# Turning the last normalized rows by DMA, and three shifts of order, in a long forward and backward kernel

## The chip, the cores and the metric

The kernel runs on one core of a Trainium2 chip. The metric is device time in microseconds (us). Before the change three runs took 1935.72, 1935.73 and 1937.65 us, median 1935.73. The run whose profile is shown took 1934.85 us; its span, from the first to the last instruction, is 1933.1 us, at a granted TensorE clock of 0.999.

The core has five engines that run in parallel, each through its own list of instructions in order: PE (TensorE, matmuls), DVE (VectorE) and ACT (ScalarE) for elementwise work, POOL (GpSimd) and SP (SyncE), which here mostly issue transfers. Transfers run on 16 DMA engines. An instruction that needs another engine's result waits for a semaphore, and everything behind it on its own engine waits with it.

## The reference, cut to what matters

The forward pass over x (2048 rows of 1024, bf16) is

```
xn = layernorm(x)
kv = shift(k) * v                     # shift: 4 taps per channel along the rows
y  = causal_conv(kv, ssm_k) + kv * D  # length 2048, by FFT in the reference
s  = xn * y
bm = ((xn @ w_gate) * (xn @ w_up)) @ w_down
out = x + s * silu(bm)
```

The kernel must give `out` and the gradients with respect to x, k, v, the shift taps, ssm_k, D and the three weight matrices for a given grad_out. The widths are 1024 model channels and 3584 inner channels.

## The kernel before, in words

The 2048 rows are 16 blocks of 128. Weights and activations stay bf16; sums are in PSUM, in f32.

**First stage, layer norm.** The rows come in six groups, `chunks`: one block, one, two, and then three groups of four (first blocks 4, 8 and 12). `ln_load` loads a group's rows on SP's queue, `layer_norm` takes mean and variance on DVE, a root on ACT, and normalizes in place (L584, L582, L585). The normalized rows lie with rows on the partitions; the matmuls need the 1024 channels on the partitions. So each block is turned: eight 128x128 transposes on PE (L591 for the first two blocks, L599 for the others) into a PSUM tile `tr`, and a copy from there into `XNT`, alternately on ACT (L601) and on DVE (L603). XNT is four tiles of four blocks; it lies in the big buffers U0 to U3, which the profile, like all of these, calls U. The rows of the three groups of four lie in U4, U6 and U7 until other data take these buffers. SP also stores turned h (below).

**Gate and up projections.** `gu_unit` takes a slab of 256 inner channels and a group of blocks: per block eight matmuls of 128x512 into `psg` (L642), a cast to `gut` by ACT (L644), and a store. The product of both halves, `hN`, is made on DVE a unit later, stored by POOL, and some units later turned on PE (L669), copied on ACT (L670) and stored by SP as `HTd`. There are 14 slabs. Slabs 0 and 1 are partly worked while the layer norm still runs; slab 1 on the last two groups, and all others, come after it, and call `tick` after each block.

**Forward convolution.** It is a generator, `conv_forward`, whose pieces are mixed into the projections. Channels go in eight blocks `ds` of 128. For every second ds, `shift` forms kv of 256 channels on DVE from k and v (loaded by POOL), in eight steps of 2.3 us; its running sum takes U6. The transforms of kv and of ssm_k are matmuls with cosine and sine tables (`psF`, L235), copied to `SP` tiles by ACT (L257, L295), and combined on DVE (tiles W, KX, HX); then a product, and an inverse transform (`inv_dft`, or `inv8` for ds 2 and 5), whose sums are on DVE and whose matmuls are `psY`. The first half-transforms of the next ds (`half`, two calls) are put on PE's list by `ahead`, once in the middle of the inverse transform (`mid`) and once behind its second reading (`after_read`), about one DVE step later. The name SP stands both for this tile and for the engine SyncE; the text says which.

`tick` counts blocks from -5, and `pump` advances the generator to the share of its planned cost that belongs to the count; from count 0 on it follows the blocks. These costs only set the order in which instructions are written out. Once they are written, each engine runs its own list, and in this stage the lists of the convolution are kept in that order.

**What comes after.** Down projection (`psbm`), gating of the output, and the backward passes of the projections, the convolution and the layer norm follow, with their own generator for the backward convolution. The change doesn't touch them.

Of the kernel before, what the change touches and what calls it, by code (L numbers as in the profile page):

```python
# [19 lines left out]
def build_kernel(  # L20
# [11 lines left out]
    nc = tc.nc  # L32
    P = 128
# [11 lines left out]
    def nat(ap2d):  # L45
        return ap2d.rearrange("(c u r) d -> u c r d", c=2, u=P, r=8)

    xq = nat(A_q.flatten_outer_dims())
# [11 lines left out]
    def ld(out, in_):  # L60
        return nc.sync.dma_start(out=out, in_=in_)
# [3 lines left out]
    def st(out, in_):  # L65
        ins = nc.gpsimd.dma_start(out=out, in_=in_)  # L66
        if PINQ[0]:
            tc.keep_in_program_order(ins)
        return ins
# [17 lines left out]
    def pool(name, bufs=1, side=None, space=None):  # L87
        kw = dict(name=name, bufs=bufs, reuse_waits="tile")
        if side:
            kw["side"] = side  # L90
        if space is not None:
            kw["space"] = space
        return tc.alloc_tile_pool(**kw)
# [118 lines left out]
    def tt(o, a, b, op):  # L212
        pinned(V.tensor_tensor(o, a, b, op))  # L213
# [292 lines left out]
    def u8(i, pat="p (a x) -> p a x", **kw):  # L506
        return U[i][:].rearrange(pat, **kw)

    XNT = [u8(q, a=DC) for q in range(4)]
# [9 lines left out]
    def keep_busy(n):  # L519
        for i in range(n):  # L520
            mm = nc.tensor.matmul(busy[:, i % 4, :], ident[:], ident[:], start=True, stop=True)
        return mm
# [19 lines left out]

    def ln_load(b0, n, x4):
        c, r0 = divmod(b0, 8)
        ld(x4[:, 0:n, :], xq[:, c, r0:r0 + n, :])

    tr_ln, act_copy = [None], [None]

    def layer_norm(b0, n, x4):
        def small(name, dt=F32):  # L550
            return lns.tile([P, 4], dt, name=name)[:, 0:n]
        mv = lns.tile([P, 4, 2], F32, name="mv")[:, 0:n, :]
        for i in range(n):
            bst = lns.tile([P, 2, 6], F32, name="bst")
            for hh in range(2):
                V.bn_stats(out=bst[:, hh, :], in_=x4[:, i, hh * 512:(hh + 1) * 512])  # L556
            V.bn_aggr(out=mv[:, i, :], in_=bst[:])
        var_b = small("var_b", BF16)
        V.tensor_copy(var_b, mv[:, :, 1])
        vpe = small("vpe", BF16)  # L560
        V.tensor_scalar(vpe, var_b, EPS, None, op0=ADD)
        r0_ = small("r0_")
        with tc.issue_after(act_copy[0].ins) if act_copy[0] is not None else nullcontext():
            root = nc.scalar.activation(r0_, vpe, ACT.Sqrt)
        mean_b = small("mean_b", BF16)
        V.tensor_copy(mean_b, mv[:, :, 0])
        rr0 = small("rr0")
        V.reciprocal(rr0, r0_)
        mean_f = small("mean_f")
        V.tensor_scalar(mean_f, mean_b, -1.0, None, op0=MUL)  # L570
        q0 = small("q0")
        tt(q0, vpe, rr0, MUL)
        r1 = small("r1")
        tt(r1, r0_, q0, ADD)
        sq_b = small("sq_b", BF16)
        V.tensor_scalar(sq_b, r1, 0.5, None, op0=MUL)
        V.reciprocal(RSTD[:, b0:b0 + n], sq_b)
        for i in range(n):
            b = b0 + i
            q, qi = divmod(b, 4)  # L580
            if n == 4 and i < 2:
                nc.scalar.activation(x4[:, i, :], x4[:, i, :], ACT.Identity, bias=mean_f[:, i:i + 1])  # L582
            else:
                V.tensor_scalar(x4[:, i, :], x4[:, i, :], mean_f[:, i:i + 1], None, op0=ADD)  # L584
            last = V.tensor_scalar(x4[:, i, :], x4[:, i, :], RSTD[:, b:b + 1], None, op0=MUL)  # L585
            if b < 2:
                for hh in range(2):
                    ps = ps_st.tile([P, 4, P], BF16, name="tr")
                    for dc in range(4):
                        d0 = (4 * hh + dc) * P  # L590
                        tr_ln[0] = nc.tensor.transpose(ps[:, dc, :], x4[:, i, d0:d0 + P], ident[:])  # L591
                    act_copy[0] = nc.scalar.copy(out=XNT[0][:, 4 * hh:4 * hh + 4, b * P:b * P + P], in_=ps[:])
                if b == 0:
                    with tc.issue_after(tr_ln[0].ins):
                        keep_busy(10)
                continue
            ps = ps_st.tile([P, DC, P], BF16, name="tr")
            for dc in range(DC):
                tr_ln[0] = nc.tensor.transpose(ps[:, dc, :], x4[:, i, dc * P:(dc + 1) * P], ident[:])  # L599
            if i % 2 == 0:  # L600
                act_copy[0] = nc.scalar.copy(out=XNT[q][:, :, qi * P:(qi + 1) * P], in_=ps[:])  # L601
            else:
                V.tensor_copy(XNT[q][:, :, qi * P:(qi + 1) * P], ps[:])  # L603
        c, r0 = divmod(b0, 8)
        return last, root, st(xnn[:, c, r0:r0 + n, :], x4[:, 0:n, :])
# [69 lines left out]
    INV8 = (2, 5)  # L675
# [4 lines left out]
    def conv_forward():  # L680
        S_ = conv_state

        def load_kv(dp, c):
            S_["k", dp] = krow
            if dp > 0 or c == 0:
                for i in range(2) if dp == 0 else (c,):
                    cld_k(krow[:, i], i, dp)
            if dp > 0 or c == 1:
                for i in range(2) if dp == 0 else (c,):
                    v = U[4][:, 2048 * i:2048 * i + 2048].rearrange("p (a x) -> p a x", a=8)  # L690
                    cld_v(v, i, dp * 256, 256)
# [43 lines left out]
        def kvs(ds):  # L735
            return S_["kvt", ds // 2][:, :, ds % 2 * P:(ds % 2 + 1) * P]
# [17 lines left out]
        cs = pool("cs", 1)  # L754
# [4 lines left out]
        def half(ds, x, i, first=None):  # L759
            if (ds, int(first is not None)) not in EIGHT:  # L760
                return fwd4_half(x, i, cf, ps_cv, first)
            SP = cf.tile([P, 2, 2, 512], F32, name="SP", bufs=2)
            fwd8_half(x, i, SP, ps_cv, first, True)
            return SP
# [34 lines left out]
        for ds in range(8):  # L799
            yield 0.5  # L800
            if ds % 2 == 1 and ds < 7:
                with tc.issue_after(S_["kst"].ins):
                    for c in range(2):
                        load_kv(ds // 2 + 1, c)
            D0 = Dz[:, ds * P:(ds + 1) * P]
            sph = []
            KX = cx.tile([P, 16, 256], BF16, name="KX")
            HX = cs.tile([P, 16, 256], BF16, name="HX", bufs=2)
            own_room = lambda X: X[:].rearrange("p a x -> p (a x)").bitcast(F32).rearrange("p (a x) -> p a x", a=8)[:, 0:4]
            eight = (ds, 1) in EIGHT  # L810
            if ds == 0:
                yield from transform(0, 1, sp, HX, own_room(KX), lambda i: sph.append(half(0, kvs(0), i)), nop)
            else:
                yield from transform(ds, 0, sp, KX, own_room(HX), lambda i: sph.append(half(ds, S_["hx"], i, D0)), nop)
                S_["kst"] = st(KFd[ds], KX[:])
            next(tl, None)
            room = cf.tile([P, 4, 256], F32, name="room", tag="hx")[:] if eight else None
            yield from transform(ds, int(ds > 0), sph, HX if ds else KX, room, nop1 if eight else lambda c: h_rows(ds + 1, c),
                                 lambda: next(tl, None))
            if ds == 0:  # L820
                S_["kst"] = st(KFd[0], KX[:])
            if eight:
                h_rows(ds + 1, 0)
            turned(HX, 1, 0, 1)
            yield 1.3
            if eight:
                h_rows(ds + 1, 1)
            if ds == 7:
                cf.release()
                S_["forward"] = False  # L830
            st(HFd[ds], HX[:])
            yield from product(KX, HX, KX, cs, False, 0)
            if ds % 2 == 1 and ds < 7:
                yield from shift(ds // 2 + 1)
            sp = []

            def ahead():
                if ds < 7:
                    sp.append(half(ds + 1, kvs(ds + 1), len(sp)))
            yield from (inv8 if ds in INV8 else inv_dft)(KX, HX, cs, ahead, ahead)  # L840
            S_["G", ds] = HX
            tl = tail(ds)
        yield 6.0
# [62 lines left out]
    cnt = [-5]  # L906
    NT = 24 * 8.0 + 14

    def tick(by=1):
        cnt[0] += by  # L910
        if cnt[0] == -4:
            pump((SHIFT_W + 4.05) / F_TOTAL)
        if cnt[0] >= 0:
            pump((SHIFT_W + (F_TOTAL - SHIFT_W) * (cnt[0] + 5) / (NT + 2)) / F_TOTAL)

    pump((SHIFT_W + 3.95) / F_TOTAL)
# [341 lines left out]
    for bp in range(1, 8):  # L1258
        ht, ht_ld = load_ht(bp) if bp > 2 else (ht1, ht2)[bp - 1]
        if bp in (3, 5, 7):  # L1260
            q = (bp - 3) // 2
# [361 lines left out]
```

## Time and profile before

| | busy us | share of the span |
|---|---|---|
| PE | 1909.7 | 99% |
| DVE | 1542.9 | 80% |
| ACT | 639.1 | 33% |
| POOL | 329.0 | 17% |

The table is the mean of stages with different limits. In the first 60 us, layer norm and first slabs, PE is busy 53.66 us and DVE 56.15; from 320 to 540 us, projections with convolution, 218.01 and 210.60 of 220; from 540 to 1300 us, 758.92 and 613.09 of 760. A wait in the profile's lists is time in which an engine stood idle until the named producer had finished. Matmuls are pipelined: one of 128x512 is listed with 379 ns, but a run of eight takes 1.73 us, 216 ns each. DMA lines give the time from issue to landing, which contains waiting behind other transfers.

### The profile page before, as it was taken

The page shows a single profiled execution, that of the slowest core. Times are in us where ns is not written, and L with a number is a line of the kernel's source. Part 1 is how long each engine was busy: PE and PEld are TensorE (multiplying, and loading weights), DVE is VectorE, ACT ScalarE, POOL GpSimd, SP SyncE. Part 2 cuts the span into 40 slices and gives each one's busy share as a digit, 9 for nine tenths or more (in the row PEclk, how much of TensorE's full clock was granted, in tenths as well). Part 3 has the DMA queues.
Part 4 walks back from the last instruction along what each step waited for, and adds up shares of the span by engine and source line. Part 5 has one row for each costly group of instructions (what it writes and reads, how often), then busy time and mean ns, then how long its engine had stood idle before and what let it go on. Part 6 is the DMA issues. An engine that isn't in the chain of part 4 may idle for free.

```text
span 1933.1 us, 27373 instructions
## 1 busy us (share of the span) xinstructions
PE 1909.7 (99%) x10860; PEld 1033.0 (53%) x10994; DVE 1542.9 (80%) x1720; ACT 639.1 (33%) x942; POOL 329.0 (17%) x461
## 2 busy tenths in 40 slices
PE   8999999999999999999999999999999999999999
PEld 5555555555544447666666666664444444444444
DVE  9999999999937555888899999999996403388883
ACT  5854555556423224333222222221222102011113
POOL 4121211201112220000122122021121101011111
PEclk9999999999999999999999999999999999999999
DMA  8876765767979987666788788575787999889873
GB/s 294 265 243 223 254 212 195 253 212 264 309 215 324 311 271 263 213 216 197 265 249 258 242 241 277 186 275 187 213 255 176 167 206 212 154 183 189 191 204 132
DMA packets 451216, 444.43 MB, mean 230 GB/s; under 512 B 268784, under 2 KB 371340, under 8 KB 436624
## 3 DMA queue, kind: packets, MB, share of 16 engines
q1 hardware_dynamic: 394704, 243.36, 46.8%
q0 software_dynamic: 40064, 169.95, 27.3%
q10 hardware_dynamic: 16320, 29.36, 4.1%
q8 instruction: 86, 1.41, 0.3%
q14 instruction: 42, 0.34, 0.1%
HBM read 194.00 MB, written 185.64 MB: 196 GB/s over the span
## 4 chain that ended last, share of the span: by engine, by line
PE 88%; DVE 9%; issue 2%; ACT 1%; DMA 0%; DVEq 0%; ACTq 0%
PE psb L1331 20%; PE psx L1461 20%; PE psg L642 12%; PE psb L1314 10%; PE psbm L961 10%; PE psb L1409 9%; PE psF L235 3%; DVE W L213 2%; DVE U L213 1%; DVE KX L213 1%; DVE bst L556 1%; PE psY L438 1%; PE tr L669 1%; PE psY L449 1%; PE psY L1108 1%
## 5 line engine op out<-in xcount | busy, mean ns | idle before, releaser
L642 PE MATMUL psg<-wslab,U 128*128 128x512 bf16 x1735 | 401.8, 379 | 3.8 <-ACT U L644 0.5
L1331 PE MATMUL psb<-U,U 128*128 128x512 bf16 x1792 | 397.1, 379 | 0.0
L1461 PE MATMUL psx<-U,dgut 128*128 128x512 bf16 x1505 | 331.0, 379 | 1.6
L1461 PEld LDWEIGHTS <-dgut 128*128 128x128 bf16 x1792 | 175.3, 98 | 211.4
L1331 PEld LDWEIGHTS <-U 128*128 128x128 bf16 x1792 | 175.3, 98 | 198.0
L642 PEld LDWEIGHTS <-U 128*128 128x128 bf16 x1792 | 173.0, 98 | 186.5 <-issue 1.9
L1314 PE MATMUL psb<-wdt,U 128*128 128x256 bf16 x1792 | 205.6, 273 | 0.0
L1314 PEld LDWEIGHTS <-U 128*128 128x128 bf16 x1792 | 175.3, 98 | 29.2
L1409 PE MATMUL psb<-U,U 128*128 128x512 bf16 x797 | 175.9, 379 | 0.9
L1336 ACT CAST wb<-psb 128x512 bf16<-128x512 f32 x112 | 65.5, 585 | 315.5 <-PE psb L1331 304.8
L213 DVE TENSOR_TENSOR W<-W 128x1024 f32<-128x1024 f32 (+1 forms) x168 | 165.4, 1001 | 3.6
L961 PE MATMUL psbm<-U,ht 128*128 128x512 bf16 x658 | 145.0, 379 | 0.7
L1409 PEld LDWEIGHTS <-U 128*128 128x128 bf16 x896 | 87.5, 98 | 104.5
L644 ACT CAST gut<-psg 128x512 bf16<-128x512 f32 x156 | 91.1, 587 | 129.1 <-PE psg L642 124.7
L1493 ACT ACTIVATE dx_t<-dxn 128x1024 bf16<-128x1024 f32 x15 | 15.9, 1057 | 320.1 <-DVE dxn L213 320.1
L961 PEld LDWEIGHTS <-ht 128*128 128x128 bf16 x672 | 65.6, 98 | 78.6
L213 DVE TENSOR_TENSOR U<-U,dht 128x2048 bf16<-128x2048 bf16 x56 | 68.3, 1221 | 47.0 <-ACT dht L1316 46.9
L1160 DVE SCALAR_TENSOR_TENSOR dkp<-dkT,kT 128x1024 bf16<-128x1024 bf16 (+2 forms) x64 | 78.4, 1224 | 32.6 <-DMA dkT<-DKSHd 30.8
L1316 ACT CAST dht<-psb 128x512 bf16<-128x512 f32 x112 | 65.6, 586 | 116.4 <-PE psb L1314 116.4
L213 DVE TENSOR_TENSOR dxn<-psx,dxna_t 128x1024 f32<-128x1024 f32 x15 | 18.3, 1222 | 85.6 <-PE psx L1461 82.4
L66 POOL DMA_DIRECT2D Hd<-hN x54 | 37.1, 688 | 264.8 <-DVE hN L213 262.4
L1440 ACT CAST wbs<-psb 128x512 bf16<-128x512 f32 x51 | 29.8, 585 | 145.1 <-PE psb L1409 134.1
(256 smaller groups left out, 2464.6 us busy)
## 6 DMA issues: line engine op xcount, KB each, us to landing
U<-GUd SPq DMA_DIRECT2D x28, 1024.0 KB, 7.5
DGd<-U SPq DMA_DIRECT2D x28, 1024.0 KB, 5.3
GUd<-gut ACTq DMA_DIRECT2D x39, 512.0 KB, 6.4
out_dram<-wb SPq DMA_DIRECT2D x112, 128.0 KB, 4.0
U<-Hd SPq DMA_DIRECT2D x14, 1024.0 KB, 6.7
Hd<-hN POOLq DMA_DIRECT2D x54, 256.0 KB, 5.0
HTd<-hT SPq DMA_DIRECT2D x52, 256.0 KB, 3.6
ht<-HTd SPq DMA_DIRECT2D x6, 1536.0 KB, 10.9
```

Of the source, the lines that this page charges most:

```text
L213: pinned(V.tensor_tensor(o, a, b, op))
L235: mm = nc.tensor.matmul(ps[:, k].rearrange("p (c d) -> p c d", c=2), T[:, r, k, :], xr[:, r], start=(n == 0), stop=(n == len(rs) - 1 and ( ...
L642: gu_mm[0] = nc.tensor.matmul(ps[:], XNT[q][:, dc, qi * P:(qi + 1) * P], w[:, dc].rearrange("p a f -> p (a f)"), start=(dc == 0), stop=(dc ...
L644: nc.scalar.copy(out=gut[:, :, i], in_=ps[:].rearrange("p (a f) -> p a f", a=2))
L961: mm = nc.tensor.matmul(ps[:, dh * 512:(dh + 1) * 512], ht(fc)[:, i * P:(i + 1) * P], WD[fc // 4][:, fc % 4, dh * 512:(dh + 1) * 512], sta ...
L1160: ins = V.scalar_tensor_tensor(prod[:].rearrange("p r d -> p (r d)")[:, lo:H], dkT[:, 0, lo:H], 1.0, kT[:, 0, 13 + m + lo:13 + m + H], op0 ...
L1314: nc.tensor.matmul(ps[:, x * SLW:(x + 1) * SLW], DBMT[2 * hf + g][:, dc, (b % 4) * P:(b % 4 + 1) * P], wdt[:, dc, :], start=(dc == 0), sto ...
L1316: nc.scalar.copy(out=dht[:, 2 * e:2 * e + 2].rearrange("p b f -> p (b f)"), in_=ps[:])
L1331: nc.tensor.matmul(ps[:], XN[b // 4][:, b % 4, dc * P:(dc + 1) * P], dgus[b // 8][:, :, b % 8], start=(b == 0), stop=(b == NB - 1))
L1336: nc.scalar.copy(out=wb[:, dc % 2].rearrange("p a f -> p (a f)"), in_=ps[:])
L1409: nc.tensor.matmul(ps, h[:, f, b, :], DBM[b // 4][:, b % 4, dh * 512:(dh + 1) * 512], start=(b == 0), stop=(b == NB - 1))
L1461: nc.tensor.matmul(ps[:, dh * 512:(dh + 1) * 512], t[n][:, f, i * P:(i + 1) * P], WGU[n][:, f, dh * 512:(dh + 1) * 512], start=(n == 0 and ...
```

## The change

Four edits:

1. The first block of rows is loaded as two transfers of 512 columns each, in place of one.
2. For the fifth and sixth groups of rows (b0 of 8 and 12), the eight transposes on PE and the copy of every block are left out. In their place stands one transposing DMA per block on SP's queue, from the normalized rows in SBUF to XNT in SBUF: eight transfers of 128x1024 bf16.
3. For odd ds, those whose next ds works on a freshly shifted kv, the first half-transform is no longer put on the list at `mid` but at `after_read`, and the second one after the end of the inverse transform.
4. `pump` follows the blocks from count -2 in place of 0.

```diff
 def ln_load(b0, n, x4):
     c, r0 = divmod(b0, 8)
-    ld(x4[:, 0:n, :], xq[:, c, r0:r0 + n, :])
+    if b0 == 0:
+        for hh in range(2):
+            ld(x4[:, 0, hh * 512:hh * 512 + 512], xq[:, c, 0, hh * 512:hh * 512 + 512])
+    else:
+        ld(x4[:, 0:n, :], xq[:, c, r0:r0 + n, :])
...
             continue
+        if b0 >= 8:
+            nc.sync.dma_start_transpose(out=XNT[q][:, :, qi * P:(qi + 1) * P], in_=x4[:, i, :])
+            continue
         ps = ps_st.tile([P, DC, P], BF16, name="tr")
...
-        yield from (inv8 if ds in INV8 else inv_dft)(KX, HX, cs, ahead, ahead)
+        yield from (inv8 if ds in INV8 else inv_dft)(KX, HX, cs, ahead if ds % 2 == 0 else None, ahead)
+        if ds % 2 == 1:
+            ahead()
...
-    if cnt[0] >= 0:
+    if cnt[0] >= -2:
         pump((SHIFT_W + (F_TOTAL - SHIFT_W) * (cnt[0] + 5) / (NT + 2)) / F_TOTAL)
```

## The prediction

> **What bounds the kernel now.** I read the page first, then the windows by stage, then the waits of PE, then the timeline of PE and of DVE around the places that the change touches, last the DMA issues.
>
> ```profile
> PE 1909.7 (99%) x10860; PEld 1033.0 (53%) x10994; DVE 1542.9 (80%) x1720; ACT 639.1 (33%) x942; POOL 329.0 (17%) x461
> ...
> 0.00:60.00 60.00, 53.66 (x395) 31.38 (x401) 56.15 (x155) 36.46 (x58) 27.23 (x43) 1.00 0.91 304
> ...
> 180.00:200.00 20.00, 17.62 (x95) 9.66 (x95) 18.45 (x13) 8.96 (x12) 2.57 (x4) 0.91 0.52 177
> ...
> 320.00:540.00 220.00, 218.01 (x1320) 121.21 (x1343) 210.60 (x195) 116.98 (x166) 32.75 (x46) 1.00 0.75 252
> 540.00:1300.00 760.00, 758.92 (x4601) 447.66 (x4618) 613.09 (x671) 228.64 (x341) 129.99 (x183) 1.00 0.77 250
> ```
>
> The first line is busy time of each engine over the span of 1933.1 us: PE has only 23.4 us in which it does nothing. The windows (stretch, then busy time of PE, PEld, DVE, ACT, POOL, then clock, DMA share, GB/s) say where these lie: 6.3 us in the first 60, 2.4 in 180:200, almost none after 540. So behind 540 us nothing is to be had except by moving everything earlier, and what the change does before 540 moves all that follows by the same amount. But DVE is busy 56.15 of 60 and 210.60 of 220 there: from 53.6 to 533 us it runs the shift and the forward convolution almost without a break. PE and DVE limit this stage together, and one cannot run far ahead of the other.
>
> ```profile
> PE psF L235 <- DVE kv L213: 3.2, 2, 2.3
> PE tr L599 <- DVE U L585: 2.3, 4, 0.8
> ...
> 36.39 0.39 PE L669 MATMUL tr<-ident,hN_s 128*128 128x128 bf16 x4
> 37.49 0.62 PE L599 MATMUL tr<-ident,U 128*128 128x128 bf16 x8 [0.71 <-DVE U L585]
> 37.95 0.38 PE L642 MATMUL psg<-wslab,U 128*128 128x512 bf16 x1
> 38.28 1.51 PE L599 MATMUL tr<-ident,U 128*128 128x128 bf16 x24
> 39.85 3.19 PE L642 MATMUL psg<-wslab,U 128*128 128x512 bf16 x14
> ...
> 48.43 0.62 PE L599 MATMUL tr<-ident,U 128*128 128x128 bf16 x8 [0.64 <-DVE U L585]
> 48.88 0.38 PE L642 MATMUL psg<-wslab,U 128*128 128x512 bf16 x1
> 49.22 1.51 PE L599 MATMUL tr<-ident,U 128*128 128x128 bf16 x24
> ```
>
> The first two lines are PE's waits (total us, times, longest): the matmuls on a freshly shifted kv, and the transposes that wait for a normalized row. The rest is PE's timeline around the last two groups of rows: start, length, what, and in brackets PE's idle time.
>
> **What the Trainium skill says.** "VectorE: DVE Perf Modes", section "The three transpose paths", gives 390 ns for TensorE and 1309 ns for the DMA crossbar, both for one 128x128 block. The trace has the TensorE ones pipelined, 24 in the 1.57 us from 38.28 to 39.85, 65 ns each. "Advanced Engine Details and Errata", section "X-Bar Transpose (TRN2)", calls transposing DMAs as fast as ordinary ones. The trace has them only from DRAM (dkT, as large as one block of rows here: issue 1.29 us, landing 3.6 us); none reads SBUF. "DMA: Bandwidth & Descriptors", section "Queues, rings and completion order", has each DMA engine go round the queues that have work, a packet at a time, so a transpose on SP's queue shares with POOL's loads. The trace agrees: small stores of SP land very late in this stretch.
>
> ```profile
> HTd<-hT_s SPq DMA_DIRECT2D x2, 128.0 KB, 9.1
> k<-in_A_k_dram POOLq DMA_DIRECT2D x4, 704.0 KB, 10.5
> dkT<-DKSHd SPq DMA_TRANSPOSE x16, 3.6
> ...
> 53.61 2.29 DVE L213 TENSOR_TENSOR U<-k,Wbc 128x4096 bf16<-128x4096 bf16 x1
> ...
> 72.45 0.69 DVE L213 TENSOR_TENSOR hN<-gut 128x1024 bf16<-128x1024 bf16 x1
> 76.94 0.69 DVE L213 TENSOR_TENSOR hN<-gut 128x1024 bf16<-128x1024 bf16 x1 [3.81 <-ACT gut L644]
> ```
>
> (DMA lines: KB each, median us from issue to landing; dkT has no size there, its tile is 128x1024 bf16, 256 KB.)
>
> **The change, part by part.**
>
> *First rows in halves.* DVE starts its first statistics at 3.60 us, 1.17 us after it ran dry, waiting for the load. Half the data lands a little sooner; against that SP spends another 0.43 us of issue before the weight slabs. The start is a chain on DVE (17.07 us busy of the first 20), so what DVE gains moves on, while a slab 0.4 us later is absorbed by PE's waits for DVE just behind. Bounds: 0.5 us won, 0.2 lost; I take 0.3 won.
>
> *Transposes of the last two groups.* PE loses 64 transposes. In the timeline they fill 37.49 to 37.95, 38.28 to 39.85, 48.43 to 48.88 and 49.22 to 50.78: 4.0 us, and the waits in front, 0.71 and 0.64, go too. Together 5.4 us. DVE loses four copies of 0.68 us (2.7), ACT four of 1.0.
>
> What is added: eight transposing DMAs on SP, in the order of SP's queue after the fourth and after the sixth store of turned h. The last two groups are the fifth and sixth of rows. The first four wait for rows that DVE normalizes from 36.94 to 38.6, then take at least 1.3 us each. PE needs these rows only after the 64 matmuls of the group before: it began them at 48.43 less the wait and five matmuls, 46.7 us, so at 44 us without the group's own transposes and wait (2.7), and then a row every 1.73 us (8 matmuls). Landing at about 40 to 47, they are in time. The second four follow rows normalized from 47.88 on; two copies fewer and the earlier start make it 46.4. PE began its matmuls on them at 57.41 and had done the four blocks at 64.31; without stall it now begins at 57.4 - 5.7 = 51.7. But from 46 to 58 us POOL's k and v loads fill the DMA engines (share 1.04 in that window; 0.33 in 38:40). A store of 128 KB on SP took 9.1 us there. Good end: first landing at 53, the rest 1.3 us apart; PE then ends the group at 53 + 4 x 1.73 = 59.9, 4.4 earlier than before. Bad end: first landing 46.4 + 9 = 55.4, then half the engines, 2.6 us each, so 63.2 for the fourth and 64.9 for the end, 0.6 later than before. I take the middle, 1.9 us earlier: of 5.7 us won, 3.8 come back as PE waiting for the DMA.
>
> Behind these on SP stand stores of turned h (nobody waits soon) and the third slab's load, issued at 64.51 when its buffer comes free: no loss.
>
> The same 2 MB also delay others. k's last load landed at 53.3 in the trace, just ahead of DVE's first shift multiply at 53.61. Eight transposes are some 10 us of all engines; I let k land 1 to 4 us later. The first shift multiply also overwrites the fifth group's x buffer, now read by DMA; those should have landed by 47. POOL waits for k too (4.77 us, until 50.58), with the stores of the products hN behind it, which nobody misses for some us. DVE could start at 50.6 and starts at about 56; kv, 18.9 us on, ends near 75. There is some room: DVE stood idle 3.81 us at 73.1 in any case. PE reached the kv matmuls at 78.20. In the new order they stand some 2.2 us sooner and PE is 1.9 earlier: 74.1. So about 0.9 us of new wait.
>
> *Pace sooner.* The order of DVE now has the first sums W ahead of the product hN, for which it idled those 3.81 us. This costs no instruction, and fills that gap with work of the 480 us chain. It wins PE nothing by itself; it lets DVE follow a PE that comes earlier. I book 0.5 us of the small waits around 75 to 85. Zero is the low end, 1 the high one.
>
> *Transforms one step later.* Behind the shift, the two halves for the next channel block are put on PE's order one and two DVE steps later (2.3 and 2.8 us), behind more psg matmuls. The wait for kv was 2.3 at 187 and about 1 at 306: 3.2 us in total, of which nearly all goes. The danger is the other end: DVE needs the first half's result right behind the inverse transform. It was PE that ran ahead at these places, by 2.3 us and more, so the result should be there. Bounds: 3.2 won, or 1 if DVE waits instead; I take 3.2.
>
> *Sum.* 0.3 + 1.9 - 0.9 + 0.5 + 3.2 = 5.0 us off the profiled span, 1933.1 to 1928.1. The run that was profiled took 1934.85, and the three timed ones have a median of 1935.73; the same 5.0 off that median is 1930.7 us.
>
> **The rivals.**
>
> A. Everything lands in time: 0.3 + 5.4 + 3.2 + 0.5 = 9.4 us, 1926.3 us. For it: the DMA share of 0.33 in 38:40, enough for the first group. Against: 46 to 58 us, as above.
>
> B. DVE becomes the bound. The transposes give nothing, k comes 4 us late, and the won kv waits turn into PE waiting for hN or for the sums, since DVE has only 14 us without work between 53 and 533 (465.71 busy of 480). Then nothing to 2 us remain: 1934.5 us. For it: that figure. Against: 2.7 us of copies leave DVE, and the 3.81 us gap is fillable.
>
> C. Slower: an SBUF source makes the crossbar slow. The eight queue on SP one behind another from 37 us. With s us each, the last lands at 37 + 8s + 2 and PE ends the group 1.7 later. Against 64.3 before, and with 3.5 won elsewhere, it decides at s = 3.4 us. By the skill's 1309 ns for each of eight blocks in a row s would be 10.5 and the loss over 50 us; dkT's landings, eight such blocks in 3.6 us, speak against that, so if it comes I expect s near 5: the last at 79, PE 16 us late, 1948 us.
>
> That the change doesn't do what it says is excluded for the transposes: the new order of PE has 64 fewer.
>
> **How the numbers follow.** Chances: the forecast 0.38 (1927.5 to 1933), A 0.27 (1924 to 1928), B 0.22 (1932 to 1938), C 0.13. Some 0.2%, 3.9 us, is what a measurement of this kernel can tell from no change. All of A and nearly 0.9 of the forecast's case lie below 1931.9: 0.60. Within: the rest of the forecast's and most of B: 0.23. Slower: C and the upper end of B: 0.17. Range: from A's middle less its uncertainty to B's end, 1924.5 to 1938.0, C left out.
>
> **What the profile after would show.** No transposes of groups five and six on PE (64 fewer); DMA_TRANSPOSE on SP at 37 to 52 us. If I am right: PE waits for them (releaser DMA U<-U) of 3 to 5 us, only on the last group; the kv wait below 0.5 us; DVE's 3.8 us idle before hN gone; k's landing near 56. If A: no such wait. If C: SP issues of over 3 us each. I am wrong if PE shows new waits on SP (the tile), W or hN in 80 to 530 us that add up to over 3 us, or if DVE idles after the inverse transforms.

## The result, and the profile after

The changed kernel took 1955.53 us (median of four runs, 1953.29 to 1959.11), beside 1935.72 us for the kernel before on the same chip (four runs, 1935.56 to 1937.65). The ratio is 1.0102, with a 95% interval of 1.0084 to 1.0119: some 20 us slower, where 5 us faster was forecast. The profiled span is 1951.5 us against 1933.1, 18.4 longer.

The page first: the engines' busy time, the granted clock in 40 slices, and PE's costliest group in this stage (busy us and mean ns, then idle us before it and what ended most of it). The last line is the same group before the change.

```profile
PE 1909.0 (98%) x10796; PEld 1029.0 (53%) x10930; DVE 1541.4 (79%) x1716; ACT 635.5 (33%) x938; POOL 329.9 (17%) x461
...
PEclk9799999999999999999999999999999999999999
...
L649 PE MATMUL psg<-wslab,U 128*128 128x512 bf16 x1735 | 405.5, 383 | 27.3 <-DMA U<-U 18.7
```

```profile
L642 PE MATMUL psg<-wslab,U 128*128 128x512 bf16 x1735 | 401.8, 379 | 3.8 <-ACT U L644 0.5
```

PE has lost its 64 transposes, from 10860 to 10796 instructions, yet is busy for as long as before. The last two lines say why: the matmuls that consume the turned rows cost 405.5 us in place of 401.8, and PE stood idle 27.3 us in front of them where before it was 3.8. Of these, 18.7 wait for `U<-U`, the new DMA. The clock has a 7 in the second slice of 49 us, so part of these matmuls ran slower.

PE's and DVE's waits give the number of times and the longest.

```profile
PE psg L649 <- DMA U<-U: 18.7, 3, 11.5
PE psg L649 <- ACT gut L651: 4.5, 2, 3.4
```

```profile
DVE U L213 <- DMA U<-U: 22.1, 1, 22.1
```

The waits for kv (3.2 us before) no longer stand in PE's list. Two new ones do: the transposing DMAs, and a wait for a cast of 3.4 us at about 534 us, as long as the kv waits were together. DVE waits for the DMAs too, once, for 22.1 us. The timeline of SP's own queue shows where the transfers stood (start, length, what).

```profile
37.40 28.36 SPq L602 DMA_TRANSPOSE U<-U  x4
65.86 1.07 SPq L61 DMA_DIRECT2D HTd<-hT_s  x2
67.02 9.99 SPq L602 DMA_TRANSPOSE U<-U  x4
77.11 2.26 SPq L61 DMA_DIRECT2D HTd<-hT_s  x2
83.05 0.37 SPq L540 DMA_DIRECT2D wslab<-in_B_w_up_dram  x1
```

To issue the first four transposes took SP 28.36 us, 7 us each. They were issued at 37.40, 39.02, 41.66 and 53.97 and landed at 43.0, 58.3, 69.6 and 73.5. The second four, for rows that had been normalized by 48.6, could not be issued until 67.02; they landed at 75.2 to 80.9. The view of this source line has the shortest, the median and the longest issue in ns:

```profile
L602 SPq DMA_TRANSPOSE U<-U x8: 1255/2052/12217, 37.4 to 75.7; - x8
```

The shortest are the last three, 1.25 to 1.33 us each at 73 to 77 us; the longest are the third and the fourth, about 12 us each. The timelines of PE and of DVE show what that did.

```profile
41.55 5.34 PE L649 MATMUL psg<-wslab,U 128*128 128x512 bf16 x24
58.37 3.59 PE L649 MATMUL psg<-wslab,U 128*128 128x512 bf16 x8 [11.48 <-DMA U<-U]
61.76 1.06 PE L676 MATMUL tr<-ident,hN 128*128 128x128 bf16 x8
...
69.68 0.61 PE L649 MATMUL psg<-wslab,U 128*128 128x512 bf16 x1 [6.86 <-DMA U<-U]
...
73.55 1.90 PE L649 MATMUL psg<-wslab,U 128*128 128x512 bf16 x8 [0.31 <-DMA U<-U]
...
82.86 0.22 PE L733 MATMUL tr<-ident,U 128*128 128x128 bf16 x1
```

```profile
51.00 0.68 DVE L174 TENSOR_SCALAR mm<-mm 128x1024 int32<-128x1024 int32 x1
73.82 2.29 DVE L213 TENSOR_TENSOR U<-k,Wbc 128x4096 bf16<-128x4096 bf16 x1 [22.13 <-DMA U<-U]
```

PE resumes each time a block lands: 58.3, 69.6, 73.5. All three are blocks of the first four; PE does not wait for the second four. The last line of PE's is the same place in the work as one before the change, the transposes that follow the last group's matmuls:

```profile
64.31 0.22 PE L726 MATMUL tr<-ident,U 128*128 128x128 bf16 x1
```

82.86 less 64.31 is 18.5 us, and the spans differ by 18.4. So all of the loss is made by 83 us, and behind that point nothing is earned or lost in sum: the kv waits of 3.2 us are gone, and the 3.4 us at 534 have come. DVE's wait has a second cause in the same transfers: the shift's first multiply writes into U6, which holds the fifth group's rows, and these are free only when the DMAs have read them, at about 73.5.

**Why they land late.** The DMA view of 52 to 62 us gives each queue's packets, MB and the time that these took as a share of 16 engines. A packet is the piece of a transfer that the profile lists. q0 is POOL's, q1 SP's, q10 ACT's.

```profile
DMA packets 1263, 2.37 MB, mean 237 GB/s; under 512 B 603, under 2 KB 603, under 8 KB 1249
...
q0 software_dynamic: 485, 1.74, 71.2%
q10 hardware_dynamic: 262, 0.51, 14.1%
q1 hardware_dynamic: 516, 0.13, 9.8%
...
U<-U SPq DMA_TRANSPOSE x2, 23.8
```

And that of 73 to 78 us, where POOL's loads are over:

```profile
q1 hardware_dynamic: 4329, 1.17, 112.5%
...
U<-U SPq DMA_TRANSPOSE x3, 3.3
```

In the first window the two queues have nearly equal numbers of packets, 516 and 485, but q1's are of 0.13 MB / 516 = 252 bytes and q0's of 3.6 KB. A transpose moves its rows in 256-byte packets; the k and v loads and the stores of normalized rows (XNd) on POOL go in packets of some KB. With a packet of each in turn, the transposes get 7% of the bytes of the two queues. A block of 256 KB is about 1,000 such packets; at 52 a us it takes some 20 us. In the second window SP's queue alone moves 4329 packets in 5 us, 866 a us, and a block lands in 3.3 us. This agrees with what the Trainium skill states in "DMA: Bandwidth & Descriptors", "Queues, rings and completion order": an engine goes round its queues a packet at a time.

In other windows of this run the counts are not equal: from 50 to 58 us q1 has 576 packets and q0 247, and from 41 to 45 us q1 has 42 and q0 121, although the second transpose had been issued at 39.02. So taking turns is not all that slowed the transfers here. The same turns are seen far more cleanly in the kernel with k loaded earlier, below.

POOL loses too. From 50 to 58 us the windows view has 360 GB/s before the change and 159 after (clock, DMA share and GB/s are the last three columns; first before, then after):

```profile
50.00:58.00 8.00, 7.77 (x58) 4.34 (x56) 8.00 (x8) 7.79 (x11) 3.35 (x5) 1.00 1.04 360
```

```profile
50.00:58.00 8.00, 0.00 (x0) 0.00 (x0) 1.65 (x3) 0.00 (x0) 2.02 (x3) 0.50 1.07 159
```

PE and ACT have nothing to do in those 8 us, and DVE has 1.65 us of work. k's last load landed at 59.9 in place of 53.3.

### The profile page after: what moved, and what is told of

Same layout as the page of the kernel before. It is cut to its first block, busy times and chain, and to the rows that moved or that the text cites. A ratio compares the mean times of both kernels' runs of the same rounds, so it can differ in the third digit from the quotient of the medians.

```text
span 1951.5 us, 27259 instructions
## 1 busy us (share of the span) xinstructions
PE 1909.0 (98%) x10796; PEld 1029.0 (53%) x10930; DVE 1541.4 (79%) x1716; ACT 635.5 (33%) x938; POOL 329.9 (17%) x461
## 4 chain that ended last, share of the span: by engine, by line
PE 82%; DVE 11%; issue 2%; DMA 2%; ACT 1%; SPq 1%; POOL 0%; ACTq 0%; DVEq 0%; POOLq 0%
PE psb L1340 20%; PE psx L1470 20%; PE psb L1323 10%; PE psbm L970 10%; PE psb L1418 9%; PE psg L649 8%; DVE W L213 3%; DVE KX L213 2%; PE psF L235 2%; DVE HX L213 1%; DVE U L213 1%; DMA U<-U 1%; DVE m L213 1%; DVE hN L213 1%; DVE bst L560 1%
## 5 line engine op out<-in xcount | busy, mean ns | idle before, releaser
L649 PE MATMUL psg<-wslab,U 128*128 128x512 bf16 x1735 | 405.5, 383 | 27.3 <-DMA U<-U 18.7
```

Source lines behind the costliest of these rows:

```text
L649: gu_mm[0] = nc.tensor.matmul(ps[:], XNT[q][:, dc, qi * P:(qi + 1) * P], w[:, dc].rearrange("p a f -> p (a f)"), start=(dc == 0), stop=(dc ...
```

## The experiments

My theory: the loss is edit 2 alone, and comes from transposes that share the DMA engines with POOL's queue. Rivals: the crossbar is slow in itself with an SBUF source (C of the prediction, S in the expectations below); the total load of the DMA engines is too high, whatever queue it is on; another edit loses.

### Without the transposing DMAs

The changed kernel, last two groups turned on PE again.

```diff
-            if b0 >= 8:
-                nc.sync.dma_start_transpose(out=XNT[q][:, :, qi * P:(qi + 1) * P], in_=x4[:, i, :])
-                continue
```

> The changed kernel with the transposes of the fifth and sixth groups back on PE; the other three edits stay. All theories put the loss on the transposing DMAs, so it must vanish here. By the prediction's terms: wait for kv 3.2 us gone, 0.3 for the first rows, 0.5 for the pace: about 1931.7 us. If the other three edits are worth nothing: 1935.7; if they have a part in the loss: above 1937.

Measured: 1931.73 us (17 runs, 1930.71 to 1933.41), beside 1935.41 before; ratio 0.9980 [0.9973, 0.9987]. Edits 1, 3 and 4 are 3.7 us faster; edit 2 costs 24 us on top of them. This is the fastest kernel here. Between the profiled spans of the changed kernel and of this one, 1951.5 and 1929.8, lie 21.7 us. Of these, 18.7 are made by the transposes that follow the last group's matmuls (82.86 there, 64.14 here); most of the rest falls at about 534 us, where the changed kernel waits 3.4 us for a cast, this one 1.5. PE's waits:

```profile
PE tr L603 <- DVE U L589: 2.4, 4, 1.0
PE psg L646 <- ACT gut L648: 1.5, 1, 1.5
...
PE psF L235 <- ACT SP L295: 1.3, 2, 1.0
PE psg L646 <- DMA wslab<-in_B_w_gate_dram: 1.2, 2, 0.7
```

No kv among them, and the waits for a normalized row (first line) are back with the transposes.

### The transposing DMAs alone

Before, with edit 2 only.

```diff
+            if b0 >= 8:
+                nc.sync.dma_start_transpose(out=XNT[q][:, :, qi * P:(qi + 1) * P], in_=x4[:, i, :])
+                continue
```

> The kernel before with the transposing DMAs alone. Theory (the transposes crawl behind POOL's loads of k and v) and rival S (a transpose from SBUF is slow in itself) both expect PE waits for DMA U<-U of 17 to 20 us and the time of the changed kernel plus what the other edits win: 1955 to 1959 us. If the loss needs the interplay with the other edits, it is well below 1950.

Measured: 1963.37 us (four runs, 1960.59 to 1965.18), ratio 1.0136 [1.0117, 1.0156]. It loses more than forecast, 28 us: the DMAs land later still, and the kv waits remain. PE's waits:

```profile
PE psg L645 <- DMA U<-U: 28.6, 3, 16.4
...
PE psF L235 <- DVE kv L213: 3.2, 2, 2.3
```

### k and v held back

The changed kernel; POOL reads the last turned block first, so its loads of k and v start only when all transposes have landed.

```diff
-        if i == 3:
-            with tc.issue_after(xsts[4].ins):
+        if i == 4:
+            landed = const.tile([P, 2], BF16, name="landed")
+            cp = nc.gpsimd.tensor_copy(landed[:], XNT[3][:, 0, 4 * P - 2:4 * P])
+            with tc.issue_after(cp.ins):
                 for _ in range(2):
                     next(conv)
```

> The changed kernel with POOL's loads of k and v held back until the last transpose has landed (a small copy on POOL reads it first). Theory: with those loads away, the eight transposes go at 1.2 to 1.6 us each, the first four issued by 43 us, and PE waits for U<-U under 2 us in all (18.7 before). The shift then starts when k has landed, near 67 us in place of 73.8, and PE waits for kv instead, 10 to 18 us: 1945 to 1952 us. Rival S: issue of the first four still takes over 20 us and PE still waits over 15 us for U<-U.

Measured: 1955.81 us (four runs, 1953.62 to 1965.22), ratio 1.0111 [1.0086, 1.0137]. Nothing was won, where 4 to 11 us were expected. The profile is that of the slowest of the four runs, 1965.22. In it the waits for the DMAs fell to 10.0 us, but not below 2. POOL's stores of the normalized rows were still there (40.08 to 46.97 and 49.82 to 61.80 us); that they hold up the transposes as the loads did is likely, but this run alone doesn't show it. And k, issued only at 71.08, made DVE late, so that PE waited 9.5 us for kv instead. So it isn't enough to shorten PE's waits for the transposes: DVE must be able to start as well.

```profile
PE psg L649 <- DMA U<-U: 10.0, 3, 7.8
PE psF L235 <- DVE kv L213: 9.5, 1, 9.5
```

### k loaded earlier

The changed kernel, k's load put ahead of the first transposes; v as it was.

```diff
+        if i == 1:
+            with tc.issue_after(xsts[-1].ins):
+                next(conv)
...
-                for _ in range(2):
-                    next(conv)
+                next(conv)
```

> The changed kernel with the loads of k moved ahead, to the second chunk (issue near 22 us in place of 39), v where it was. Theory: only v (1 MB) and stores are left beside the transposes, so PE waits for U<-U fall from 18.7 to below 7 us and the time is 1932 to 1941 us. Rival S: no difference, 1953 to 1957 us.

Measured: 1947.23 us (five runs, 1944.12 to 1958.21), ratio 1.0065 [1.0041, 1.0088]: 8 us won, where 15 to 23 were expected. PE waited 13.6 us once, where I had expected below 7 in all. Of the first four, two, issued at 39.52 and 41.19, landed only at 61.14 and 62.73, right behind 59.6, when POOL's queue (v and both XNd stores) had run empty; the second four then were issued in 5.60 us, 1.4 each:

```profile
38.08 23.54 SPq L602 DMA_TRANSPOSE U<-U  x4
...
62.85 5.60 SPq L602 DMA_TRANSPOSE U<-U  x4
```

Rival C falls here: from the same SBUF source, a block takes 1.4 us of issue once POOL is silent. And this run shows the turns. While the second and the third transpose were under way, the queues moved these packets from 43 to 49, 49 to 55 and 55 to 61 us:

```profile
q0 software_dynamic: 189, 1.42, 95.7%
q1 hardware_dynamic: 195, 0.05, 5.2%
...
q0 software_dynamic: 394, 1.44, 76.0%
q1 hardware_dynamic: 399, 0.10, 8.5%
...
q0 software_dynamic: 490, 2.13, 89.2%
q1 hardware_dynamic: 507, 0.12, 9.8%
```

SP's queue gets one packet for one of POOL's in all three. POOL's are of 7.5, 3.7 and 4.3 KB (MB over packets), and the transposes' pace goes with them: 33, 67 and 85 packets a us. In all, the DMA engines move about as much as before the change, 361 GB/s in the same 50 to 58 us:

```profile
50.00:58.00 8.00, 0.00 (x0) 0.00 (x0) 0.70 (x1) 0.00 (x0) 1.97 (x3) 0.50 1.06 361
```

So the turns slow the transposes, but they don't explain the 159 GB/s of the changed kernel.

### The same transfers, in line on SP

If total load were the cause, it would not matter on which queue k, v and XNd stand. Here these transfers, of the same size, are on SP's queue between the transposes, so that little of POOL's is left to alternate with them. Their order is not quite the same: k is issued from 45.92 in place of 39.39, behind the first four, and v from 64.89 in place of 42.70, behind all eight.

```diff
-            cld(t[u:u + n, a:], rows(u, n, a))
+            (ld if dp == 0 else cld)(t[u:u + n, a:], rows(u, n, a))
...
-            cld(t[:, a:a + 4, :], vin[:, c, a:a + 4, d0:d0 + w])
+            (ld if (d0, w) == (0, 256) else cld)(t[:, a:a + 4, :], vin[:, c, a:a + 4, d0:d0 + w])
...
-        return last, root, st(xnn[:, c, r0:r0 + n, :], x4[:, 0:n, :])
+        return last, root, (ld if b0 >= 8 else st)(xnn[:, c, r0:r0 + n, :], x4[:, 0:n, :])
...
-                for _ in range(2):
-                    next(conv)
+                next(conv)
+        if i == 4:
+            with tc.issue_after(xsts[5].ins):
+                next(conv)
```

> The changed kernel with the same loads of k and v, and the two stores of rows, at their places but on SP's queue, in line with the transposes in place of beside them on POOL's. Theory: the same bytes in the same stretch, but served one after the other, so the first four transposes land by 45 us and PE does not wait for them; the last four come behind k, near 56 to 62 us, PE waits 3 to 8 us; 1932 to 1940 us. Rival: if it is the total load on the DMA engines that counts, not the queue, the first four are as late as in the changed kernel (last landing near 70 us) and the time stays near 1955.

Measured: 1938.26 us (12 runs, 1935.15 to 1943.49), ratio 1.0010 [1.0001, 1.0018]. SP's queue:

```profile
37.47 7.78 SPq L602 DMA_TRANSPOSE U<-U  x4
...
53.58 10.19 SPq L602 DMA_TRANSPOSE U<-U  x4
```

The profile is that of the fastest run, 1935.15. The first four are issued in 7.78 us, 1.9 each, against 28.36, and land by 47.34. From 40 to 46 us SP's queue moves 3391 packets, where the changed kernel's moved 602. Against the total load speaks the windows view (first the changed kernel, then this one):

```profile
46.00:58.00 12.00, 0.89 (x5) 0.20 (x2) 5.44 (x13) 2.35 (x4) 2.87 (x4) 0.63 1.07 167
```

```profile
46.00:58.00 12.00, 7.58 (x52) 4.14 (x50) 5.22 (x11) 9.02 (x13) 2.68 (x3) 0.91 1.10 296
```

The DMA engines move more bytes here, with the transposes far ahead of where they were. So it isn't the number of bytes in this stretch that held them. How much the line on one queue does, and how much the later k and v, this run doesn't tell apart; that POOL's packets are taken in turns with SP's is shown by the run before. What remains, 7.7 us of PE waiting once, is queueing: the second four stand behind k and the store of rows. One thing comes with the move: from 50 to 58 us SP's 3184 packets, nearly all of k, have 1.58 MB, 0.5 KB each, where POOL sent its loads in packets of 3.5 KB and more. So the size of the packets changed here with the queue, for the same load.

### A quiet queue

The changed kernel with k on SP behind the rows' loads, both XNd stores on SP behind the transposes, v on POOL held until the last block has landed, and the shift's products in a fixed order behind it.

```diff
+            (ld if dp == 0 else cld)(t[u:u + n, a:], rows(u, n, a))
...
+        return last, root, (ld if b0 >= 8 else st)(xnn[:, c, r0:r0 + n, :], x4[:, 0:n, :])
...
+                with tc.issue_after(last.ins):
+                    tt(prod, k[:, :, 3 - j:11 - j, :], wb(j), MUL)
...
+    next(conv)
...
+        if i == 4:
+            landed = const.tile([P, 2], BF16, name="landed")
+            cp = nc.gpsimd.tensor_copy(landed[:], XNT[3][:, 0, 4 * P - 2:4 * P])
+            with tc.issue_after(cp.ins):
+                next(conv)
```

> The changed kernel with POOL's queue kept almost empty while the transposes run: k is loaded on SP's queue right behind the rows, the two stores of normalized rows stand on SP's queue behind the transposes that they used to run beside, and v's load waits on POOL until the last transpose has landed. Theory (a transpose's small packets take turns with POOL's large ones): issue of 1.3 us each, PE waits for U<-U under 2 us, so the 5.4 us that the prediction gave to the transposes show up: 1926 to 1930 us, below the kernel with PE transposes (1931.7). Rival S (slow from SBUF in itself, or from the two transfers reading the same rows): waits of 10 us and more, 1942 to 1956 us.

Measured: 1936.83 us (14 runs, 1930.99 to 1945.81), ratio 1.0003 [0.9989, 1.0017]. No loss against before, but the gain that I expected did not come: it is 5 us behind the kernel that turns on PE (the kernel before took 1935.63 us beside this one and 1935.41 beside that one). PE's waits:

```profile
PE psg L649 <- DMA U<-U: 4.5, 2, 2.9
PE psx L1473 <- DMA dgut<-DGd: 4.2, 1, 4.2
```

The first four were issued in 8.46 us and landed from 42.39 to 48.54, the others from 55.59 to 62.29: 2.1 to 2.4 us of issue each, slower than the 1.3 that dkT's take. Even so PE waited 4.5 us, close to the 5.4 us that the transposes cost on PE. The second line, at 1660 to 1664 us, lies far outside the change, and none of the other profiles has it. It is 4.2 of the 5.0 us between the profiled spans, 1934.8 and 1929.8. In the stage itself the two kernels are thus within 1 us of each other in these profiles; whether the slower of the 14 runs all have this wait isn't known.

### Edits 3 and 4 alone

Edit 3 alone on the kernel before:

```diff
-            yield from (inv8 if ds in INV8 else inv_dft)(KX, HX, cs, ahead, ahead)
+            yield from (inv8 if ds in INV8 else inv_dft)(KX, HX, cs, ahead if ds % 2 == 0 else None, ahead)
+            if ds % 2 == 1:
+                ahead()
```

> The kernel before with the third edit alone. By the prediction PE's waits for kv (3.2 us) vanish: 1932.2 us, ratio 0.998. If PE then only meets the next DVE-bound wait, the time is unchanged and the waits stand under another name.

Measured: 1933.89 us (21 runs, 1930.76 to 1949.59), ratio 0.9989 [0.9979, 1.0000]. The profiled span is 1930.5, 2.6 under before. The kv wait is gone and the first of PE's waits are now

```profile
PE tr L599 <- DVE U L585: 2.3, 4, 0.8
PE psg L642 <- ACT gut L644: 1.8, 1, 1.8
```

the second of which, at 516 us, is new: part of the 3.2 comes back there.

Edit 4 alone on the kernel before:

```diff
-        if cnt[0] >= 0:
+        if cnt[0] >= -2:
```

> The kernel before with the fourth edit alone. By the prediction 0.5 us at most: DVE's 3.81 us idle near 73 us is filled, PE's waits for kv stay or shrink. If DVE is the true bound of the stretch, all of the 3.8 us is won: 1931.9 us.

Measured: 1935.08 us (21 runs, 1932.46 to 1939.28), ratio 0.9994 [0.9988, 1.0001], which can't be told from nothing. DVE's idle 3.81 us ahead of hN at 73 us are gone, and one of 4.32 stands at 133.6 us.

Edit 1 was not run alone. In the kernel without the transposing DMAs DVE's wait for the first rows is 0.6 us where it was 1.17, but in the changed kernel, which has edit 1 too, it is 1.1. PE's 1.2 us for a slab stand in the profile of edit 2 alone as well, without edit 1. What edit 1 is worth can't be read from these runs.

## Why the prediction was wrong

**The step that failed** is the cost of the first four transposes, which the prediction put at nothing: "Landing at about 40 to 47, they are in time". The second, third and fourth block came 15, 27 and 31 us after the first, which landed at 43.0, and all of PE's 18.7 us of waiting for the DMAs stand in front of these three (11.48, 6.86 and 0.31). The DMA share of 0.33 in 38 to 40 us, which spoke for their being in time, was over when the second block was issued at 39.02: POOL's store of normalized rows began at 38.86.

**The price behind it** failed as well: "Bad end: first landing 46.4 + 9 = 55.4, then half the engines, 2.6 us each", and with it the term "of 5.7 us won, 3.8 come back", which was booked for the second four alone. It divided the DMA engines by time. The section on queues that the prediction itself names divides them by packets, and the packets of a transpose are 14 times smaller than POOL's. The trace has 516 packets of 252 bytes in 10 us, which makes some 20 us for a block in place of 2.6. For the second four the 3.8 us did not come: they were held back on SP until POOL was nearly done, and PE's list has no wait for them.

**What was counted out.** I had said that the first shift multiply overwrites the fifth group's rows, and put it aside since they should have landed by 47. They landed at 73.5, and DVE stood 22.13 us. That every step of SP waits until its queue takes the next transfer was in the working only for rival C; in the run it kept four blocks of ready rows from being issued until 67.02.

**Rival C** had the right sign and size (1948 us, decision at 3.4 us of issue a block) for the wrong reason: a block takes 1.3 to 2.5 us of issue from SBUF when POOL is quiet (1.4 each in the kernel with k loaded earlier, once POOL was silent). Its statement "SP issues of over 3 us each" is what the trace shows for the first four, 7.1 each, and would have been read as its confirmation; the last three of the same run, at 1.25 to 1.33, and the kernel with k loaded earlier tell the two apart.

**Rivals A and B** fell with the same step: of the first four only the first block landed in time, and DVE did not become the bound, it stood still for the same DMAs.

**What held.** The 5.4 us of PE's transposes did leave the list, and the kv wait of 3.2 went as forecast. For edits 1, 3 and 4 the sum was 0.3 + 3.2 + 0.5 = 4.0 us; they measured 3.7. By parts it is less sure: by its ratio edit 3 gave 2.1 us (0.0011 of 1935.7; the interval reaches from 0 to 4.1), in the spans 2.6, and edit 4 something between 2.3 won and 0.2 lost. With parts so uncertain, that the sum came out so close may be luck.

**A reading.** The 23.4 us in which PE does nothing, before the change, are too many: that trace lists 134 matmuls fewer, 10860 in place of 10994, than the one of edit 4 alone, whose PE is idle 16.9 us (1934.4 less 1917.5). No term of the sum rests on it.

**Open.** That the two queues take turns packet by packet is shown by the counts of the kernel with k loaded earlier. Not explained is what else held the changed kernel: the 42 packets of SP's queue from 41 to 45 us, and the drop of all queues together to 159 GB/s from 50 to 58, which that kernel, with the same turns, doesn't have. So how the 24 us divide between the turns and these stretches is not known. Nor was it varied alone that the XNd stores read the same rows as the transposes.

## What to carry to other kernels

Before you move work to a transfer, look at which queues are busy in that window and at the packet size of each; a transfer in small packets beside a queue of large ones gets a share by packets, here 7% of the bytes of the two queues. If it has to be there, put the large transfers on the same queue, in an order that you choose, or elsewhere in time. Here that took the loss away, but won nothing over PE: 1938.26 and 1936.83 us, beside 1931.73 with the transposes on PE. And ask who overwrites the source: a DMA that reads a buffer late holds up its next writer as well as its reader.

## What was not expected of the hardware

- Four transposing DMAs of 256 KB blocked SP for 28.36 us beside POOL's traffic, and two stores and four further blocks with it; with that traffic behind them on one queue it was 7.78.
- One packet for one: 189, 394 and 490 packets of POOL's beside 195, 399 and 507 of SP's in three stretches of 6 us, whatever the size of POOL's.
- After 11.48 us of idleness PE's first eight matmuls took 3.59 us in place of 1.90, and the clock of 50 to 62 us was 0.50. "TensorE: Matmul & The Clock Gate", Part 1, gives half the clock after an idle stretch of about 3.4 us. The trace agrees on the half; where the limit lies was not measured. A wait thus costs more than its length: 1.7 us more here.
